# Cosformer attention and a gelu MLP on one core: batch 0's first chunk by halves, fp32 idle matmuls, a 128-column selector

## The chip, the core and the metric

The kernel runs on one core of a Trainium2 chip. A core has five engines that run side by side: TensorE (PE, matmuls; its weight loads are shown apart as PEld), VectorE (DVE), ScalarE (ACT), GpSimd (POOL) and SyncE (SP, which here only issues DMAs). PE reads SBUF and writes PSUM; DVE and ACT carry results from PSUM to SBUF. The metric is device time in microseconds, the median of several executions. Beside it stands one profiled execution, whose trace all views of the profile come from.

## What is computed

Eight batches of a linear attention with eight heads, 576 positions and head size 64, and then a two-layer MLP on the 4608 rows of the result. Cut to what matters:

```python
def phi(x, c, s):
    r = np.maximum(x, 0.0)
    return np.concatenate([r * c, r * s], axis=-1)
q_p, k_p = phi(q, cos_w, sin_w), phi(k, cos_w, sin_w)
kv = np.einsum('bhsf,bhsd->bhfd', k_p, v)
z = np.sum(k_p, axis=2)
num = np.einsum('bhsf,bhfd->bhsd', q_p, kv)
den = np.einsum('bhsf,bhf->bhs', q_p, z)[..., None] + 1e-06
x = (num / den).transpose(0, 2, 1, 3).reshape(4608, 512)
h = x @ w_in                       # 512 x 2048
g = h / (1.0 + np.exp(-1.702 * h))
out = g @ w_out                    # 2048 x 512
```

## The kernel before

The order of the instructions is written out by hand, and each engine takes its own in that order; the tile framework adds the semaphores. A tile name stands for a buffer out of a pool: PSUM has four buffers "mm" (pool pmm, one bank each) and two buffers "at" (pool pat, two banks each). A buffer is given again when its last reader is done.

Batch 0 has nothing to hide behind, and its steps stand at the end of the code (L355 to L435):

- SP issues four loads at the very start: k in two parts, then q in two parts (L62, L63). POOL waits for k's first part (the tiny copy into "gate" at L130), then issues v in two parts (heads 0 to 3 and 4 to 7, cast to bf16) and the first two of four parts of w_in (L132 to L134).
- idle(12) at L355 runs twelve matmuls on zeros before k lands; more of them stand between later steps.
- trig (L135) makes relu(x)cos and relu(x)sin of 64 positions, one instruction each, on DVE, on ACT, or, for q's last group, on POOL. There are nine groups j of k and of q. Groups 0 to 3 of q lie in its first loaded part.
- ksum(j) (L214) sums k over the positions: four matmuls with the selector "sel" of two columns. ksum_evac brings the sums to column 64 of "kvs".
- qturn_pe(c) turns two groups of q (128 positions, a chunk) on PE, and qevac(c) copies the result to qT, on DVE or ACT. Chunk 4 has one group.
- kv_mm(0, 2) and kv_mm(2, 4) (L202) make k times v for four heads each, 36 matmuls of 64 rows, into two "at" tiles; kv_evac copies them to kvs on DVE.
- den_early(0) makes chunk 0's denominators; num_mm(c) (L226) makes the numerators of eight heads, with the denominators in column 64 of each, into an "at" tile; num_div(c) on DVE adds 1e-6, takes the reciprocal and multiplies, into "xn".
- xturn_mm(c) turns xn on PE into the free columns of the same "at" tile, and xturn_evac(0, c) copies that on ACT to x. Chunk 4 goes by a DMA instead.
- part(c, fcs) makes the first w_in products of chunk c alone, four matmuls of 128 columns for each of the first four blocks fc of hidden units; gelu and the following blocks (mm1, 512 columns) come after all of them. The first is mm1(0, 4).

The other batches overlap their attention with the MLP of the batch before. SP, POOL, DVE and ACT take batch 1's loads and preparation behind batch 0's steps, in the same order as the code.

Of the kernel before, what the change touches and what calls it, by code (L numbers as in the profile page):

```python
# [9 lines left out]
F32 = mybir.dt.float32  # L10
BF16 = mybir.dt.bfloat16
AF = mybir.ActivationFunctionType
MUL = mybir.AluOpType.mult
# [6 lines left out]
def kernel(  # L20
# [40 lines left out]
    for t, src, cut in ((kf, k, 192), (qf0, q, 256)):  # L61
# [44 lines left out]

    win_r = moe_w_in.rearrange("(kc p) f -> p kc f", p=128)
    wout_r = moe_w_out.rearrange("(g p c) d -> p g c d", p=128, c=4)
    w_in_v = [t.rearrange("p k (f c) -> p k c f", c=4) for t in w_in_sb]

    def w_in_of(kc, fc):
        return w_in_v[fc // 4][:, kc, fc % 4, :]

    def load(t, src, b, eng=nc.gpsimd):
        eng.dma_start(out=t, in_=src_of(src, b))
# [5 lines left out]
                            in_=q[b, :, 512:S, :].rearrange("h p d -> p h d"))  # L121

    def load_win(g):
        nc.gpsimd.dma_start(out=w_in_sb[g], in_=win_r[:, :, ts(g, 512)])

    def load_wout(g):
        nc.gpsimd.dma_start(out=w_out_sb[:, ts(g, 4), :], in_=wout_r[:, g])
# [7 lines left out]
    def trig(dst, src, j, act=False, eng=nc.vector):  # L135
        i = src[:, :, ts(j, 64)]
        for cs, w in enumerate((cosw, sinw)):
            o = dst[:, j, :, ts(cs, 64)]
            if act:
                nc.scalar.activation(o, i, AF.Relu, scale=w[:, j:j + 1])  # L140
            else:
                eng.tensor_scalar(o, i, 0.0, w[:, j:j + 1], op0=MAX, op1=MUL)  # L142
# [24 lines left out]
    def qturn_pe(c, home=None):  # L167
        tp = pmm.tile([128, 2, NI, 128], BF16, name="mm") if home is None else home
        for j in range(2 * c, min(2 * c + 2, NS)):
            for i in range(NI):  # L170
                nc.tensor.transpose(tp[:, j % 2, i], qn0[:, j, i, :], ident)  # L171
        tps[c] = tp

    def qevac(c, act=False):
        n = min(2 * c + 2, NS) - 2 * c
        o = qT[:, :, ds(c * 128, n * 64)].rearrange("f h (j p) -> f j h p", j=n)
        i = tps.pop(c)[:, 0:n].rearrange("f j i (hh p) -> f j (i hh) p", hh=2)
        if act:
            nc.scalar.activation(o, i, AF.Copy)  # L179
        else:  # L180
            nc.vector.tensor_copy(o, i)  # L181
# [10 lines left out]
    st = {}  # L192
# [9 lines left out]
    def kv_mm(i0, i1, rhs, col, n):  # L202
        for i in range(i0, i1):
            for j in range(NS):
                for hh in range(2):
                    r = slice(hh * 64, hh * 64 + 64)
                    nc.tensor.matmul(st["kv", i][:, hh, ds(col, n)], kr[r, j, i, :], rhs(r, i, j),  # L207
                                     start=(j == 0), stop=(j == NS - 1))

    def kv_evac(i0, i1, n=65):  # L210
        o = st["kvs"][:, :, i0:i1, 0:n]
        nc.vector.tensor_copy(o, st["ps", i0].rearrange("p hh (i e) -> p hh i e", e=65)[:, :, :, 0:n])  # L212

    def ksum(j):  # L214
        if j == 0:
            st["z"] = pmm.tile([128, NI, 2], F32, name="mm")
        for i in range(NI):
            nc.tensor.matmul(st["z"][:, i], kr[:, j, i, :], sel, start=(j == 0 and i == 0),
                             stop=(j == NS - 1 and i == NI - 1))

    def ksum_evac():
        nc.vector.tensor_copy(st["kvs"][:, :, :, 64], st["z"].rearrange("f i hh -> f hh i"))

    nums = {}

    def num_mm(c):  # L226
        ps = pat.tile([128, 2, 512], F32, name="at")
        for h in range(H):
            i, hh = divmod(h, 2)
            nc.tensor.matmul(ps[:, h // 4, ds((h % 4) * 65, 65)], qT[:, h, ts(c, 128)],  # L230
                             st["kvs"][:, hh, i, 0:65], start=True, stop=True)
        nums[c] = [ps]

    def inv_of(d):
        den = small.tile([128, 2, 4], F32, name="den")
# [3 lines left out]
        return inv  # L239

    def den_early(c):
        d = pmm.tile([128, 2, 4], F32, name="mm")
        for h in range(H):
            nc.tensor.matmul(d[:, h // 4, h % 4:h % 4 + 1], qT[:, h, ts(c, 128)],
                             st["kvs"][:, h % 2, h // 2, 64:65], start=True, stop=True)
        return inv_of(d)

    def num_div(c, inv=None):
# [4 lines left out]
        xn = small.tile([128, 2, 4, 64], BF16, name="xn", bufs=4)  # L253
        nc.vector.tensor_tensor(xn, pv[:, :, :, 0:64],  # L254
                                inv.unsqueeze(3).to_broadcast([128, 2, 4, 64]), op=MUL)
        nums[c].append(xn)

    x = {}

# [9 lines left out]
    def xturn_mm(c):  # L269
        ps, xn = nums[c]  # L270
        xv = xn.rearrange("p a h e -> p (a h e)")
        for kc in range(KC):
            o = ps[:, kc // 2, ds(264 + (kc % 2) * 64, 64)].bitcast(BF16)
            nc.tensor.transpose(o, xv[:, ts(kc, 128)], ident)  # L274

    def xturn_evac(b, c):
        ps = nums.pop(c)[0]
        i = ps[:, :, 264:392].bitcast(BF16).rearrange("p a (k t) -> p a k t", k=2)
        o = x_of(b, c).rearrange("p (a k) t -> p a k t", a=2)
        nc.scalar.activation(o, i, AF.Copy)  # L280

    def xturn_dma(b, c):
# [5 lines left out]
    gT = {}  # L288
    hp = {}

    def mm1_part(b, fc, t0, t1):
        if t0 == 0:
            hp[fc] = pmm.tile([128, MT], F32, name="mm")
        for kc in range(KC):
            nc.tensor.matmul(hp[fc][:, t0:t1], w_in_of(kc, fc), x[b][:, kc, t0:t1],  # L295
                             start=(kc == 0), stop=(kc == KC - 1))

# [75 lines left out]
    ksum_evac()  # L373
    idle(1, w)
    qturn_pe(0)
    for j in (2, 3):
        trig(qn0, qf0, j, act=True)
    idle(2, w)
    qturn_pe(1)
    for j in (4, 5):  # L380
        trig(qn0, qf0, j)
    trig(qn0, qf0, 8, eng=nc.gpsimd)
    nc.gpsimd.tensor_copy(gate[0:1, 1:2], vb[0:1, 3, 0:1])
    load_win(2)
    load_win(3)
    kv_mm(0, 2, vb_rhs, 0, 64)
    qturn_pe(2)
    for j in (6, 7):
        trig(qn0, qf0, j, act=True)
    qevac(0)  # L390
    qevac(1)
    qevac(2, act=True)
    inv0 = den_early(0)
    kv_evac(0, 2, 64)
    kv_mm(2, 4, vb_rhs, 0, 64)
    kv_evac(2, 4, 64)
    qturn_pe(3)
    qevac(3, act=True)
    num_mm(0)
    num_div(0, inv0)  # L400
    num_mm(1)
    num_div(1)
    qturn_pe(4)
    qevac(4)
    idle(1)
    x_open(0)
    xturn_mm(0)
    xturn_evac(0, 0)
    num_mm(2)
    num_div(2)  # L410
    xturn_mm(1)
    xturn_evac(0, 1)

    def part(c, *fcs):
        for fc in fcs:
            mm1_part(0, fc, c * 128, c * 128 + 128)

    part(0, 0, 1, 2, 3)
    num_mm(3)
    num_div(3)  # L420
    xturn_mm(2)
    xturn_evac(0, 2)
    part(1, 0, 1, 2, 3)
    num_mm(4)
    num_div(4)
    xturn_mm(3)
    xturn_evac(0, 3)
    xturn_dma(0, 4)
    part(2, 0, 1, 2)
    part(3, 0, 1)  # L430
    part(2, 3)
    part(3, 2, 3)
# [150 lines left out]
```

## Time and profile before

| what | value |
|---|---|
| time of the kernel, median of 3 runs | 292.08 us (291.86 to 293.0) |
| the profiled execution: time | 292.75 us |
| its span, first to last instruction | 291.0 us |
| granted TensorE clock over the span | 1.000 |
| PE busy from 14.40 to 17.80 us | 2.39 of 3.40 us |
| PE busy from 17.80 to 21.70 us | 3.88 of 3.90 us |
| w_in's loads, issue to landing, least / median / most | 7.9 / 9.5 / 11.8 us |
| v's two loads of batch 0, issue to landing | 6.8 and 7.3 us |

A row of the timeline has the start, the time from the first start to the last end, the engine, the line, the operation with "output<-input", the shape and the number of instructions merged. A bracket at its end is the idle time of the engine before it and what ended it. Matmuls overlap, so the distance between two starts is what one costs, and not its duration. A row of the stage table has for each engine the busy time and the number of instructions; the figure after the engines is the share of full clock that PE was granted.

### The profile page before, as it was taken

What the parts mean: (1) busy time and instruction counts of PE and PEld (TensorE: products, weight loads), DVE (VectorE), ACT (ScalarE), POOL (GpSimd) and SP (SyncE); (2) the same over time, 40 slices, a digit from 0 to 9 for tenths busy, and PEclk for the clock granted to TensorE, in tenths of its full rate; (3) what the DMA queues carried; (4) which work ended last, traced back from release to release, by engine and by line L of the source; (5) the groups of instructions that cost most, each with busy time, mean ns of one, the idle gap of its engine ahead of it and who ended that gap; (6) DMA issues with size and microseconds to landing.
All of it is one profiled execution on the core that took longest, in us unless ns stands there. A gap on an engine that the chain in (4) does not pass through costs nothing.

```text
span 291.0 us, 5656 instructions
## 1 busy us (share of the span) xinstructions
PE 281.8 (97%) x2247; PEld 153.0 (53%) x2282; DVE 123.7 (43%) x356; ACT 133.1 (46%) x232; POOL 37.8 (13%) x71
## 2 busy tenths in 40 slices
PE   6989999999999999999999999999999999999995
PEld 2685475555555555555455545554555455544444
DVE  3872656912657354826582567156624200000000
ACT  6857564793157214721463136412651176751111
POOL 6560042301210011001100110011000100002000
PEclk9999999999999999999999999999999999999999
DMA  7999999982699877989797579846952600002322
GB/s 239 247 213 289 368 247 362 239 193 76 128 271 260 219 131 260 289 184 147 221 314 198 96 203 346 222 102 159 373 94 72 119 36 1 0 2 44 84 90 72
DMA packets 67770, 52.48 MB, mean 180 GB/s; under 512 B 47968, under 2 KB 57952, under 8 KB 67744
## 3 DMA queue, kind: packets, MB, share of 16 engines
q1 hardware_dynamic: 60320, 32.52, 47.0%
q0 software_dynamic: 7424, 19.60, 23.9%
q8 instruction: 18, 0.29, 0.4%
q14 instruction: 8, 0.07, 0.1%
HBM read 36.70 MB, written 9.44 MB: 159 GB/s over the span
## 4 chain that ended last, share of the span: by engine, by line
PE 91%; DMA 3%; ACT 2%; DVE 1%; issue 1%; SPq 1%; ACTq 0%
PE mm L332 42%; PE mm L295 37%; PE mm L312 5%; PE at L230 3%; PE at L207 3%; DMA qf<-in_q_dram 3%; ACT g L300 1%; PE at L274 1%; DVE qn L142 1%; DVE qT L181 0%; PE at L171 0%; ACT qT L179 0%; SPq L62 0%; DVE xn L254 0%; ACT xT L280 0%
## 5 line engine op out<-in xcount | busy, mean ns | idle before, releaser
L332 PE MATMUL mm<-w_out_sb,g 128*128 128x512 bf16 (+1 forms) x506 | 116.7, 372 | 1.3 <-issue 0.2
L295 PE MATMUL mm<-xT,w_in 128*128 128x512 bf16 (+1 forms) x551 | 111.9, 360 | 0.5
L300 ACT ACTIVATE g<-mm 128x512 bf16<-128x512 f32 x128 | 75.6, 598 | 31.0 <-PE mm L295 31.0
L295 PEld LDWEIGHTS <-w_in 128*128 128x128 bf16 x560 | 59.8, 113 | 50.9
L332 PEld LDWEIGHTS <-g 128*128 128x128 bf16 x528 | 48.6, 98 | 49.1
L336 ACT ACTIVATE ysb<-mm 128x512 f32<-128x512 f32 (+1 forms) x37 | 21.7, 586 | 105.9 <-PE mm L332 103.0
L340 POOL DMA_DIRECT2D out_dram<-ysb x39 | 21.3, 547 | 204.7 <-ACT ysb L336 204.7
L142 DVE TENSOR_SCALAR kr<-kf,cosw 128x256 bf16<-128x256 f32 x64 | 22.6, 353 | 29.4 <-DMA kf<-in_k_dram 29.4
L254 DVE TENSOR_TENSOR xn<-at,inv 128x512 bf16<-128x512 f32 x40 | 27.7, 691 | 1.9 <-PE at L230 0.4
L142 DVE TENSOR_SCALAR kr<-kf,sinw 128x256 bf16<-128x256 f32 x64 | 22.2, 347 | 0.0
L212 DVE CAST kvs<-at 128x520 bf16<-128x520 f32 (+1 forms) x9 | 5.6, 634 | 33.7 <-PE at L207 33.7
L236 DVE TENSOR_SCALAR den<-at 128x8 f32<-128x8 f32 x39 | 6.5, 166 | 31.4 <-PE at L230 31.4
L230 PEld LDWEIGHTS <-qT 128*128 128x128 bf16 x320 | 14.8, 97 | 8.8 <-issue 0.8
L230 PE MATMUL at<-kvs,qT 128*128 128x65 bf16 x320 | 16.1, 193 | 0.7 <-ACT xT L280 0.7
L155 DVE TENSOR_SCALAR qn<-qf,sinw 128x512 bf16<-128x512 f32 (+1 forms) x30 | 14.4, 480 | 0.0
L155 DVE TENSOR_SCALAR qn<-qf,cosw 128x512 bf16<-128x512 f32 (+1 forms) x30 | 14.3, 476 | 0.0
L312 PE MATMUL mm<-xt,w_in 128*128 128x512 bf16 x63 | 13.9, 379 | 0.1
L332 PE MATMUL mm<-w_out_sb,gl_t 128*128 128x512 bf16 x63 | 13.9, 379 | 0.1
L313 ACT ACTIVATE gl_t<-mm 128x512 bf16<-128x512 f32 x16 | 9.6, 597 | 4.2 <-PE mm L312 4.2
L207 PEld LDWEIGHTS <-kr 64*128 64x128 bf16 x576 | 9.3, 94 | 2.8 <-issue 2.5
L312 PEld LDWEIGHTS <-w_in 128*128 128x128 bf16 x64 | 7.2, 113 | 6.6
L332 PEld LDWEIGHTS <-gl_t 128*128 128x128 bf16 x64 | 6.3, 98 | 7.5
(63 smaller groups left out, 114.5 us busy)
## 6 DMA issues: line engine op xcount, KB each, us to landing
kf<-in_k_dram SPq DMA_DIRECT2D x5, 1152.0 KB, 6.7
vf<-in_v_dram SPq DMA_DIRECT2D x5, 1152.0 KB, 9.5
qf<-in_q_dram SPq DMA_DIRECT2D x5, 1024.0 KB, 5.9
out_dram<-ysb POOLq DMA_DIRECT2D x20, 256.0 KB, 3.9
out_dram<-ysb POOLq DMA_DIRECT2D x19, 128.0 KB, 3.2
kf<-in_k_dram POOLq DMA_DIRECT2D x2, 1152.0 KB, 11.3
vf<-in_v_dram POOLq DMA_DIRECT2D x2, 1152.0 KB, 15.7
w_in<-in_moe_w_in_dram POOLq DMA_DIRECT2D x4, 512.0 KB, 9.5
```

Source lines behind the costliest of these rows:

```text
L142: eng.tensor_scalar(o, i, 0.0, w[:, j:j + 1], op0=MAX, op1=MUL)
L155: nc.vector.tensor_scalar(o, i, 0.0, sc, op0=MAX, op1=MUL)
L207: nc.tensor.matmul(st["kv", i][:, hh, ds(col, n)], kr[r, j, i, :], rhs(r, i, j), start=(j == 0), stop=(j == NS - 1))
L230: nc.tensor.matmul(ps[:, h // 4, ds((h % 4) * 65, 65)], qT[:, h, ts(c, 128)], st["kvs"][:, hh, i, 0:65], start=True, stop=True)
L254: nc.vector.tensor_tensor(xn, pv[:, :, :, 0:64], inv.unsqueeze(3).to_broadcast([128, 2, 4, 64]), op=MUL)
L295: nc.tensor.matmul(hp[fc][:, t0:t1], w_in_of(kc, fc), x[b][:, kc, t0:t1], start=(kc == 0), stop=(kc == KC - 1))
L300: nc.scalar.activation(g, hp.pop(fc), AF.Gelu_apprx_sigmoid)
L312: nc.tensor.matmul(hps, w_in_of(kc, fc), xt[:, kc, :], start=(kc == 0), stop=(kc == KC - 1))
L313: nc.scalar.activation(gl_t[:, fc, :], hps, AF.Gelu_apprx_sigmoid)
L332: nc.tensor.matmul(yp[t, c0][:, c0:c1], w, w_out_sb[:, fc, c0:c1], start=(fc == 0), stop=(fc == FC - 1))
L336: nc.scalar.activation(ysb[:, c0:c1], yp[t, c0][:, c0:c1], AF.Identity)
L340: eng.dma_start(out=dst[:, c0:c1], in_=ysb[p0:p0 + n, c0:c1])
```

## The change

- The idle matmuls at the start are three on fp32 zeros (a 128x128 tile read four times over) in place of twelve on bf16 zeros; the later idles read the same bytes as bf16. Of these one stays, before qturn_pe(1); nine others go.
- The selector has 2 x 64 columns in place of 2, so that a sum stands 64 times in PSUM; ksum_evac reads the first of each.
- w_in's first part is loaded as two tiles, each with half of the input rows.
- Chunk 0 is done by halves of four heads: numerators of heads 0 to 3 right after kv_mm(0, 2), then kv_mm(2, 4), division, turn and copy of the first half, then the second; the first two blocks' w_in products of the first half stand ahead of the second half.
- qevac(0) stands on DVE between q's groups 4 and 5, q's group 7 on ACT behind qevac(1), and qevac(3) on DVE in place of ACT. den_early also makes chunk 1's denominators, in the tile of chunk 0's.
- Chunk 4 of q is turned into free columns of chunk 2's "at" tile (qturn_last) and copied on ACT (qevac_last), after num_mm(2) and ahead of num_div(2).
- The w_in products of chunks 0 to 3 stand in a new order around num_mm(3), num_mm(4) and the turns.

```diff
-    warm = const.tile([128, 512], BF16)
-    nc.vector.memset(warm, 0.0)
+    warm32 = const.tile([128, 128], F32)
+    nc.vector.memset(warm32, 0.0)
+    warm = warm32.bitcast(BF16)
...
-    sel = const.tile([128, 2], BF16)
+    sel = const.tile([128, 2, 64], BF16)
     nc.vector.memset(sel, 0.0)
     for hh in range(2):
-        nc.vector.memset(sel[hh * 64:hh * 64 + 64, hh:hh + 1], 1.0)
+        nc.vector.memset(sel[hh * 64:hh * 64 + 64, hh], 1.0)
...
-    w_in_sb = [one.tile([128, KC, 512], BF16, name=f"w_in{g}") for g in range(4)]
+    w_in0 = [one.tile([128, 2, 512], BF16, name=f"w_in0{u}") for u in "ab"]
+    w_in_sb = [one.tile([128, KC, 512], BF16, name=f"w_in{g}") for g in range(1, 4)]
...
+    def qturn_last(c_home):
+        for i in range(NI):
+            o = nums[c_home][0][:, i // 2, ds(264 + (i % 2) * 64, 64)].bitcast(BF16)
+            nc.tensor.transpose(o, qn0[:, NS - 1, i, :], ident)
+
+    def qevac_last(c_home):
+        nc.scalar.activation(qT[:, :, ds(512, 64)].rearrange("f (a h) p -> f a h p", a=2),
+                             nums[c_home][0][:, :, 264:392].bitcast(BF16).rearrange(
+                                 "f a (h p) -> f a h p", h=4), AF.Copy)
...
-    def idle(n, w=None):
+    def idle(n, w=None, t=warm):
         if w is None:
             w = pmm.tile([128, 512], F32, name="mm")
         for _ in range(n):
-            nc.tensor.matmul(w, warm[:, 0:128], warm, start=True, stop=True)
+            nc.tensor.matmul(w, t[:, 0:128], t[:, 0:128].unsqueeze(1).to_broadcast([128, 4, 128]),
+                             start=True, stop=True)
         return w
...
-    w = idle(12)
+    w = idle(3, t=warm32)
...
-    for j in (0, 1, 2):
-        ksum(j)
-    for j in (3, 6, 4, 7, 5):
-        idle(1, w)
-        ksum(j)
-    idle(1, w)
-    ksum(8)
+    for j in (0, 1, 2, 3, 6, 4, 7, 5, 8):
+        ksum(j)
```

num_mm, num_div, xturn_mm and xturn_evac get bounds for the half (heads h0 to h1, halves a0 to a1 of the tile), and mm1_part gets bounds k0 to k1 of the input blocks. From the sums on, batch 0's order was this, up to the mm1 of block 4:

```python
ksum_evac(); idle(1, w); qturn_pe(0); trig q 2, 3 (ACT); idle(2, w); qturn_pe(1)
trig q 4, 5; trig q 8 (POOL); load_win(2); load_win(3)
kv_mm(0, 2); qturn_pe(2); trig q 6, 7 (ACT); qevac(0); qevac(1); qevac(2, act=True)
inv0 = den_early(0); kv_evac(0, 2); kv_mm(2, 4); kv_evac(2, 4)
qturn_pe(3); qevac(3, act=True); num_mm(0); num_div(0, inv0); num_mm(1); num_div(1)
qturn_pe(4); qevac(4); idle(1); x_open(0); xturn_mm(0); xturn_evac(0, 0)
num_mm(2); num_div(2); xturn_mm(1); xturn_evac(0, 1)
part(0, 0, 1, 2, 3); num_mm(3); num_div(3); xturn_mm(2); xturn_evac(0, 2)
part(1, 0, 1, 2, 3); num_mm(4); num_div(4); xturn_mm(3); xturn_evac(0, 3); xturn_dma(0, 4)
part(2, 0, 1, 2); part(3, 0, 1); part(2, 3); part(3, 2, 3)
```

and becomes this:

```python
ksum_evac(); trig q 8 (POOL); load_win(2); load_win(3)
qturn_pe(0); trig q 2, 3 (ACT); trig q 4; qevac(0); trig q 5; trig q 6 (ACT)
idle(1, w); qturn_pe(1); qevac(1, act=True); trig q 7 (ACT)
kv_mm(0, 2); kv_evac(0, 2); inv0 = den_early(0); qturn_pe(2)
num_mm(0, 0, 4); kv_mm(2, 4); num_div(0, inv0, 0, 1); kv_evac(2, 4)
x_open(0); xturn_mm(0, 0, 1); xturn_evac(0, 0, 0, 1); inv1 = den_early(1); qevac(2, act=True)
num_mm(0, 4, 8); num_mm(1); mm1_part(0, fc, 0, 128, 0, 2) for fc in (0, 1)
num_div(0, inv0, 1, 2); num_div(1, inv1); xturn_mm(0, 1, 2); xturn_evac(0, 0, 1, 2)
qturn_pe(3); qevac(3); xturn_mm(1); xturn_evac(0, 1)
num_mm(2); qturn_last(2); qevac_last(2); num_div(2)
mm1_part(0, fc, 0, 128, 2, 4) for fc in (0, 1); part(0, 2, 3)
num_mm(3); num_div(3); part(1, 0); xturn_mm(2); xturn_evac(0, 2); part(1, 1, 2, 3)
part(2, 0); xturn_mm(3); xturn_evac(0, 3); num_mm(4); num_div(4); xturn_dma(0, 4)
part(2, 1, 2); part(3, 0, 1); part(2, 3); part(3, 2, 3)
```

More of the change, by code (lines that the diff above doesn't have):

```diff
@@ L108 @@
     wout_r = moe_w_out.rearrange("(g p c) d -> p g c d", p=128, c=4)
+    w_in0_v = [t.rearrange("p k (f c) -> p k c f", c=4) for t in w_in0]
     w_in_v = [t.rearrange("p k (f c) -> p k c f", c=4) for t in w_in_sb]
     def w_in_of(kc, fc):
-        return w_in_v[fc // 4][:, kc, fc % 4, :]
+        if fc < 4:
+            return w_in0_v[kc // 2][:, kc % 2, fc, :]
+        return w_in_v[fc // 4 - 1][:, kc, fc % 4, :]
     def load(t, src, b, eng=nc.gpsimd):
@@ L123, in load_win @@
     def load_win(g):
-        nc.gpsimd.dma_start(out=w_in_sb[g], in_=win_r[:, :, ts(g, 512)])
+        if g == 0:
+            for u in range(2):
+                nc.gpsimd.dma_start(out=w_in0[u], in_=win_r[:, ds(2 * u, 2), 0:512])
+        else:
+            nc.gpsimd.dma_start(out=w_in_sb[g - 1], in_=win_r[:, :, ts(g, 512)])
     def load_wout(g):
@@ L221, in ksum_evac, with num_mm @@
     def ksum_evac():
-        nc.vector.tensor_copy(st["kvs"][:, :, :, 64], st["z"].rearrange("f i hh -> f hh i"))
+        nc.vector.tensor_copy(st["kvs"][:, :, :, 64], st["z"][:, :, :, 0].rearrange("f i hh -> f hh i"))
     nums = {}
-    def num_mm(c):
-        ps = pat.tile([128, 2, 512], F32, name="at")
-        for h in range(H):
+    def num_mm(c, h0=0, h1=H):
+        if h0 == 0:
+            nums[c] = [pat.tile([128, 2, 512], F32, name="at")]
+        ps = nums[c][0]
+        for h in range(h0, h1):
             i, hh = divmod(h, 2)
@@ L241, in den_early @@
     def den_early(c):
-        d = pmm.tile([128, 2, 4], F32, name="mm")
+        if c == 0:
+            st["den"] = pmm.tile([128, 2, 2, 4], F32, name="mm")
+        d = st["den"][:, c]
         for h in range(H):
@@ L267, in x_of, with xturn_mm, xturn_evac @@
         return xt[:, :, ts(b, 64)] if c == 4 else x[b][:, :, ts(c, 128)]
-    def xturn_mm(c):
+    def xturn_mm(c, a0=0, a1=2):
         ps, xn = nums[c]
         xv = xn.rearrange("p a h e -> p (a h e)")
-        for kc in range(KC):
+        for kc in range(2 * a0, 2 * a1):
             o = ps[:, kc // 2, ds(264 + (kc % 2) * 64, 64)].bitcast(BF16)
             nc.tensor.transpose(o, xv[:, ts(kc, 128)], ident)
[L276 to L279, printed above, removed]
+    def xturn_evac(b, c, a0=0, a1=2):
+        ps = nums[c][0] if a1 < 2 else nums.pop(c)[0]
+        i = ps[:, a0:a1, 264:392].bitcast(BF16).rearrange("p a (k t) -> p a k t", k=2)
+        o = x_of(b, c).rearrange("p (a k) t -> p a k t", a=2)[:, a0:a1]
         nc.scalar.activation(o, i, AF.Copy)
@@ L289, with mm1_part @@
     hp = {}
-    def mm1_part(b, fc, t0, t1):
-        if t0 == 0:
+    def mm1_part(b, fc, t0, t1, k0=0, k1=KC):
+        if t0 == 0 and k0 == 0:
             hp[fc] = pmm.tile([128, MT], F32, name="mm")
-        for kc in range(KC):
+        for kc in range(k0, k1):
             nc.tensor.matmul(hp[fc][:, t0:t1], w_in_of(kc, fc), x[b][:, kc, t0:t1],
@@ L373 @@
     ksum_evac()
[L374 to L381, printed above, removed]
     trig(qn0, qf0, 8, eng=nc.gpsimd)
@@ L385 @@
     load_win(3)
+    qturn_pe(0)
+    for j in (2, 3):
+        trig(qn0, qf0, j, act=True)
+    trig(qn0, qf0, 4)
+    qevac(0)
+    trig(qn0, qf0, 5)
+    trig(qn0, qf0, 6, act=True)
+    idle(1, w)
+    qturn_pe(1)
+    qevac(1, act=True)
+    trig(qn0, qf0, 7, act=True)
     kv_mm(0, 2, vb_rhs, 0, 64)
+    kv_evac(0, 2, 64)
+    inv0 = den_early(0)
     qturn_pe(2)
[L388 to L391, printed above, removed]
-    qevac(2, act=True)
[L393 to L400, printed above, removed]
-    num_mm(1)
[L402 to L410, printed above, removed]
+    num_mm(0, 0, 4)
+    kv_mm(2, 4, vb_rhs, 0, 64)
+    num_div(0, inv0, 0, 1)
+    kv_evac(2, 4, 64)
+    x_open(0)
+    xturn_mm(0, 0, 1)
+    xturn_evac(0, 0, 0, 1)
+    inv1 = den_early(1)
+    qevac(2, act=True)
+    num_mm(0, 4, 8)
+    num_mm(1)
+    q3 = pmm.tile([128, 2, NI, 128], BF16, name="mm")
+    for fc in (0, 1):
+        mm1_part(0, fc, 0, 128, 0, 2)
+    num_div(0, inv0, 1, 2)
+    num_div(1, inv1)
+    xturn_mm(0, 1, 2)
+    xturn_evac(0, 0, 1, 2)
+    qturn_pe(3, q3)
+    qevac(3)
     xturn_mm(1)
     xturn_evac(0, 1)
+    num_mm(2)
+    qturn_last(2)
+    qevac_last(2)
+    num_div(2)
     def part(c, *fcs):
@@ L416, in part @@
             mm1_part(0, fc, c * 128, c * 128 + 128)
-    part(0, 0, 1, 2, 3)
+    for fc in (0, 1):
+        mm1_part(0, fc, 0, 128, 2, 4)
+    part(0, 2, 3)
     num_mm(3)
     num_div(3)
+    part(1, 0)
     xturn_mm(2)
     xturn_evac(0, 2)
-    part(1, 0, 1, 2, 3)
+    part(1, 1, 2, 3)
+    part(2, 0)
+    xturn_mm(3)
+    xturn_evac(0, 3)
     num_mm(4)
     num_div(4)
-    xturn_mm(3)
-    xturn_evac(0, 3)
     xturn_dma(0, 4)
-    part(2, 0, 1, 2)
+    part(2, 1, 2)
     part(3, 0, 1)
```

13 lines of the change are left out of this document (6 added, 7 removed).

## The prediction

> **What bounds the kernel now.** I read four views of the profile: the page's first parts, the table of stages (busy time by stretch), the timeline of TensorE (PE), and the timeline of the other engines.
>
> ```profile
> PE 281.8 (97%) x2247; PEld 153.0 (53%) x2282; DVE 123.7 (43%) x356; ACT 133.1 (46%) x232; POOL 37.8 (13%) x71
> ...
> 14.40:17.80 3.40, 2.39 (x51) 2.16 (x49) 2.78 (x8) 2.22 (x3) 3.40 (x6) 1.00 1.24 207
> 17.80:21.70 3.90, 3.88 (x77) 3.78 (x76) 2.40 (x7) 1.90 (x4) 1.14 (x3) 1.00 1.25 213
> 21.70:291.00 269.30, 264.17 (x1958) 140.19 (x1988) 109.65 (x310) 118.22 (x204) 24.85 (x44) 1.00 0.69 176
> ```
>
> PE is busy nearly all the time, and from 17.8 us on it has hardly a hole. So the change, which touches only batch 0's opening, is worth what it does to the moment when PE becomes full. In the stage table the second number of a row is PE's busy time; the 14.40 row has the last large hole.
>
> ```profile
> 11.38 0.71 PE L207 MATMUL at<-vb,kr 64*128 64x64 bf16 x36
> 12.02 0.62 PE L171 MATMUL mm<-ident,qn 128*128 128x128 bf16 x8
> 12.83 0.35 PE L244 MATMUL mm<-kvs,qT 128*128 128x1 bf16 x8 [0.19 <-DVE qT L181]
> ...
> 15.42 0.40 PE L274 MATMUL at<-ident,xn 128*128 128x128 bf16 x4 [0.32 <-DVE xn L254]
> 16.51 0.40 PE L230 MATMUL at<-kvs,qT 128*128 128x65 bf16 x8 [0.69 <-ACT xT L280]
> 16.74 0.39 PE L274 MATMUL at<-ident,xn 128*128 128x128 bf16 x4
> 16.97 1.06 PE L295 MATMUL mm<-xT,w_in 128*128 128x128 bf16 x16
> 17.86 0.41 PE L230 MATMUL at<-kvs,qT 128*128 128x65 bf16 x8
> 18.13 0.40 PE L274 MATMUL at<-ident,xn 128*128 128x128 bf16 x4
> ```
>
> The brackets are PE's holes: 0.19, 0.32 and 0.69 us, all waits for chunk 0's way through DVE and ACT. That way begins with q's second half and its POOL neighbour:
>
> ```profile
> 10.67 0.35 DVE L142 TENSOR_SCALAR qn<-qf,cosw 128x256 bf16<-128x256 f32 x1 [0.84 <-DMA qf<-in_q_dram]
> 10.94 0.57 DVE L142 TENSOR_SCALAR qn<-qf,sinw 128x256 bf16<-128x256 f32 x1
> 11.43 0.34 DVE L142 TENSOR_SCALAR qn<-qf,cosw 128x256 bf16<-128x256 f32 x1
> 11.69 0.49 DVE L142 TENSOR_SCALAR qn<-qf,sinw 128x256 bf16<-128x256 f32 x1
> 12.10 1.27 DVE L181 COPY qT<-mm 128x1024 bf16<-128x1024 bf16 x2
> ...
> 39.19 0.69 DVE L181 COPY qT<-at 128x1024 bf16<-128x1024 bf16 x1 [1.63 <-PE at L171]
> 39.91 2.11 ACT L179 ACTIVATE qT<-at 128x1024 bf16<-128x1024 bf16 x2 [1.77 <-DVE qT L181]
> ```
>
> The last two rows matter most for the forecast. Both copies read halves of one PSUM tile ("at") that PE had finished at 39.16, yet ACT began only at 39.91, released by DVE: two readers of one tile go one after the other.
>
> **The start up to 11.4 us: nothing.** Twelve bf16 idle matmuls become three fp32 ones, six idles between k's sums go, and the 36 sums get 128 columns in place of 2. The trace has no fp32 matmul. If one costs a single bf16 pass, the three take 3 x 0.43 = 1.3 us at the opening spacing (12 in 4.2 us, the first seven 0.43 apart); if four passes, 3 x 1.7 = 5.1. I take four, nearest to the twelve they replace: they end near 5.3, when the first k is ready (5.28). The Trainium skill, "FP8 and Floating Point Precision", section TensorE Precision Notes, also gives true fp32 four passes; no run here shows it yet. A sum of 128 columns costs what a 128-column transpose costs (L171, 0.056 apart), so one j is 0.22 us, and the last j starts when ACT frees it (9.35) and ends by 9.58, as before with its idle. The second half of chunk 1's transposes still waits for ACT's qn (10.89) and the first kv product for v's landing (11.34), so its start stays at 11.38. POOL issues three w_in loads where two stood, some 0.8 us more; its next work waits for q until 10.67, which covers that, as it was done by 7.7. The software queue lands in order (v 11.34 and 12.72, w_in0 15.26), so w_in0's first half should land near 14.0; it is needed at 15.0. Without the split the wait would be 0.2 us.
>
> **The chain from 10.67, step by step.** I use start-to-start distances and add 0.04 to 0.06 us for each hand-over (L171 out at 15.82, ACT 15.86; DVE done 15.37, PE 15.42) and 0.16 for a matmul's way out.
>
> 1. DVE: one pair of qn (0.76, row 10.67 to 11.43), then qevac(0) 11.43 to 12.10 (before it ended 12.77), then the second pair (0.67) to 12.78, then kv_evac(0,2), 0.37 (L212's 128x256 copy), to 13.07.
> 2. PE: den_early(0) at 12.16 (before 12.83). The later half of qturn_pe(2) waits for qn until 12.84. num_mm of heads 0 to 3 at 13.13 (half of L230's 0.24), then kv_mm(2,4), 36 in 0.52, to 13.80.
> 3. The half division has no row: between 0.37 (128x256 copy) and 0.69 (L254 whole). I take 0.42, near the same-sized copy: 13.45 to 13.87. The half turn is at 13.93. The half copy on ACT lies between 0.29 (its smallest row, cosw) and 0.60 (L280 whole); 512 elements take 0.60 and 1024 take 1.02, so 256 take about 0.38: 14.24 to 14.62.
> 4. num_mm of heads 4 to 7 writes the tile that ACT just read, so it waits until 14.67 (hole 0.43); num_mm(1) and the four first w_in matmuls run to 15.25. DVE: kv_evac(2,4) to 14.40, inv1, other half of xn 14.99 to 15.41, xn(1) to 16.02. PE: xturn_mm(0) rest 15.47, qturn_pe(3), and xturn_mm(1) at 16.08. **Before, it was at 16.74: here the change is 0.66 us ahead.**
> 5. num_mm(2) 16.30, then chunk 4's four transposes into the same "at" tile, out at 16.93. ACT copies xT(1) 16.50 to 17.10, then these transposes (128x512, 0.60) to about 17.60. DVE's den(2) reads that tile too, and in the built order it stands behind this ACT copy. So den, reciprocal, xn (0.16, 0.20, 0.69, with gaps 1.13 as from 16.94 to 18.07) run 17.64 to 18.77, and xturn_mm(2) starts at 18.83; **before 18.13**. PE has from 16.76 only 12 w_in matmuls (0.67), num_mm(3) (0.24) and four more (0.22): done 17.89, hole 0.94. This hole doesn't hang on the steps before: 0.17 + 0.04 + 0.60 + 0.04 + 1.13 + 0.06 is 2.0, the cover 1.13.
> 6. xturn_mm(2) 18.83, ACT's xT(2) to 19.85, part(2, 0) waits for it (hole 0.18); xturn_mm(3) 20.12, xT(3) to 21.14; part(3, 0) at 21.19 (hole 0.16). Before, it was at 20.58. The same 20 matmuls follow in both.
>
> Sum: 21.19 - 20.58 = +0.61 us. Counted by PE's holes after 11.4: before 0.19 + 0.07 + 0.32 + 0.69 + 0.18, with the idle in the 0.32's place 0.2 more, near 1.8; after 0.13 + 0.22 + 0.07 + 0.43 + 0.22 + 0.05 + 0.94 + 0.18 + 0.16 = 2.4. Both ways say +0.6. The gain of the early half is real, and the new wait in step 5 takes more back.
>
> On that wait the Trainium skill, "PSUM — Partial Sum Buffer", section on bank collisions, says that reads of one bank by ScalarE and VectorE must be kept apart too. By that rule the order is needed, and the sum stays; rows 39.19 and 39.91 agree (0.03 us between end and start).
>
> The profiled run took 292.75 us (span 291.0, 1.75 around it), 0.67 above the median of 292.08. So I expect 293.36 on its basis, **292.7 us** on the median's.
>
> **Bounds.** Low: half division 0.37, half copy 0.29, second qn pair without POOL beside it 0.53: -0.28, so +0.3. High: 0.69, 0.60 and 0.98 (both instructions at the slow 0.49): +0.27 + 0.22 + 0.31 up to step 4, and +0.27 for the second half division: +1.7. Own range of the forecast 292.3 to 293.8.
>
> **Rivals.**
> - *The delay is swallowed later.* Some later wait with a fixed time would eat the 0.6. For it: the last stage row has 5.1 us without PE, though matmul records are missing there. Against it: the named holes after 22 us are near 0.2, and k, w_out and q of batch 1 land two to five us ahead of their use. 292.1.
> - *Faster.* Step 4's lead of 0.66 survives, because ACT takes chunk 4's copy ahead of its turn or den(2) isn't held by it. Then xn(2) follows num_mm(2) directly: DVE is free of qevac(3) at 16.96, xn(2) ends near 18.1 in place of 18.77, and with the low bounds the sum is 0.61 - 0.67 - 0.28 - 0.2 (shorter second holes): 291.5. For it: before, den always followed its num_mm within 0.23. Against: the order of the built program and row 39.91.
> - *Slower: the clock.* PE runs its first seven idles 0.43 apart and later ones 0.22, so the full clock comes at 4.2 us, after 3 us of steady work. If three fp32 matmuls are too short (one pass, over at 2.5) or count as little work, or the sums without idles between them are too thin to hold it, PE enters the chain at half speed. Between 11.4 and 14.8 it has 2.7 us of work there, some 0.9 of which would hide in holes: +1.8 on top of 0.6, 294.5. It decides once the clock is still half at 11.4. Against it: by four passes PE works without a break until 5.3, and from 7.59 to 11.0 its work is 22 x 0.056 + 1.2 = 2.4 us, close to the 2.5 of before.
>
> **Numbers.** Forecast 0.62, swallowed 0.16, faster 0.13, clock 0.09. Around 0.5% (1.5 us) is what a measurement of this kernel tells from no change, since the three runs lie 1.1 us apart: the forecast lies inside it but for its upper end. Faster by over 0.5% needs the faster rival twice over: 0.04. Slower by over 0.5%: the clock and 0.03 of the forecast's upper end, 0.12. The rest, 0.84, is the same. Range: from 291.3, just under the faster rival, to 293.9; below it 0.06, above 0.11.
>
> **What would show it** (lines of the changed kernel). den(2) at L256 on DVE released by ACT's L198 and starting near 17.6; a hole near 0.9 us before the turn of chunk 2 (L296); xturn_mm(1) earlier than 16.74; part(3,0) near 21.2; PE's clock full before 5.3, with three fp32 matmuls ending there. The forecast is wrong if den(2) starts with num_mm(2)'s end, if PE has new holes behind 22 us, or if 128-column sums lie 0.11 apart.

## The result, and the profile after

| what | before | after |
|---|---|---|
| median of 19 runs each | 292.16 us (291.56 to 293.11) | 292.94 us (292.73 to 293.63) |
| ratio after / before | | 1.0032, 95% interval 1.0024 to 1.0041 |
| the profiled execution: time, span | 292.75, 291.0 us | 292.94, 291.2 us |
| q's and v's second parts land at | 10.64, 12.72 us | 9.78, 12.39 us |
| first 512-column matmul (mm1(0, 4)) at | 21.69 us | 21.61 us |
| from there to the end | 269.35 us | 269.54 us |

The change makes the kernel 0.8 us slower, which is 0.3%. The two profiled executions differ by only 0.2 us, because the one of before had its loads land late. That is why I compare two distances that depend far less on when loads land: **the opening**, from v's second landing to the first 512-column matmul, and **the tail**, from that matmul to the end.

The page of the changed kernel and its table of stages (for each engine busy time and number of instructions, then granted clock):

```profile
PE 282.7 (97%) x2242; PEld 153.9 (53%) x2275; DVE 124.0 (43%) x356; ACT 133.5 (46%) x234; POOL 38.6 (13%) x72
...
14.40:17.80 3.40, 2.88 (x56) 2.52 (x52) 2.41 (x6) 1.85 (x4) 3.10 (x5) 1.00 1.24 207
17.80:21.61 3.81, 3.47 (x60) 3.27 (x61) 2.30 (x7) 1.88 (x4) 1.06 (x2) 1.00 1.24 209
21.61:291.15 269.54, 264.33 (x1958) 140.17 (x1989) 109.53 (x310) 118.19 (x204) 24.51 (x44) 1.00 0.67 176
```

From 14.40 to 17.80 PE was busy for 2.39 us before and is for 2.88 now: the halves do fill the old hole. From 17.80 on there was no hole before (3.88 of 3.90), and now 0.34 us are missing. The timeline of PE shows where:

```profile
13.29 0.34 PE L266 MATMUL mm<-kvs,qT 128*128 128x1 bf16 x8
13.92 0.52 PE L251 MATMUL at<-kvs,qT 128*128 128x65 bf16 x12 [0.29 <-ACT xT L302]
...
15.39 0.40 PE L296 MATMUL at<-ident,xn 128*128 128x128 bf16 x4
15.62 0.41 PE L251 MATMUL at<-kvs,qT 128*128 128x65 bf16 x8
15.87 0.39 PE L195 MATMUL at<-ident,qn 128*128 128x128 bf16 x4
...
17.12 0.28 PE L317 MATMUL mm<-xT,w_in0b 128*128 128x128 bf16 x2
18.13 0.40 PE L296 MATMUL at<-ident,xn 128*128 128x128 bf16 x4 [0.73 <-DVE xn L277]
```

Chunk 1 is turned at 15.39 (before 16.74), chunk 2 at 18.13 as before: the lead is used up in one hole of 0.9 us (17.23 to 18.13 by starts). Part of these differences is that the loads landed earlier. Counted from v's second landing, and set against e5 (the kernel before once more, see the experiments), chunk 1's turn comes after 3.00 us in place of 3.65, and chunk 2's after 5.74 in place of 5.04: a lead of 0.65 becomes a delay of 0.70. DVE and ACT tell why:

```profile
15.56 0.69 DVE L190 COPY qT<-mm 128x1024 bf16<-128x1024 bf16 x1 [0.23 <-PE mm L180]
16.94 0.17 DVE L256 TENSOR_SCALAR den<-at 128x8 f32<-128x8 f32 x1 [0.69 <-ACT qT L198]
```

```profile
15.82 0.60 ACT L302 ACTIVATE xT<-at 128x512 bf16<-128x512 bf16 x1 [0.33 <-PE at L296]
16.32 0.59 ACT L198 ACTIVATE qT<-at 128x512 bf16<-128x512 bf16 x1
```

DVE is free at 16.25 and chunk 2's numerators have been out since 16.03. It begins chunk 2's denominators only at 16.94, when ACT is through with chunk 4's copy (L198) out of the same tile. And one place behind 22 us is new:

```profile
39.84 1.02 ACT L188 ACTIVATE qT<-at 128x1024 bf16<-128x1024 bf16 x1 [1.92 <-DVE qT L190]
41.22 1.94 ACT L188 ACTIVATE qT<-at 128x1024 bf16<-128x1024 bf16 x2 [0.36 <-ACT qT L188]
```

Before, these three copies ran without a gap:

```profile
39.91 3.03 ACT L179 ACTIVATE qT<-at 128x1024 bf16<-128x1024 bf16 x3 [1.77 <-DVE qT L181]
```

Now the second begins 0.36 us late, although what it reads is ready.

### The profile page after: what moved, and what is told of

Its sections match the earlier page's. It is cut to its first block, busy times and chain, and to the rows that moved or that the text cites. A ratio compares the mean times of both kernels' runs of the same rounds, so it can differ in the third digit from the quotient of the medians.

```text
span 291.2 us, 5650 instructions
## 1 busy us (share of the span) xinstructions
PE 282.7 (97%) x2242; PEld 153.9 (53%) x2275; DVE 124.0 (43%) x356; ACT 133.5 (46%) x234; POOL 38.6 (13%) x72
## 3 DMA queue, kind: packets, MB, share of 16 engines
HBM read 36.70 MB, written 9.44 MB: 158 GB/s over the span
## 4 chain that ended last, share of the span: by engine, by line
PE 91%; DMA 3%; ACT 3%; issue 1%; DVE 1%; ACTq 0%; POOL 0%; DVEq 0%
PE mm L354 42%; PE mm L317 36%; PE mm L334 5%; PE at L251 3%; PE at L226 3%; DMA vb<-in_v_dram 2%; ACT g L322 1%; DMA kf<-in_k_dram 1%; ACT qT L188 1%; PE at L296 1%; PE at L180 0%; DVE xn L277 0%; ACT xT L302 0%; PE mm L180 0%; DVE qT L190 0%
## 5 line engine op out<-in xcount | busy, mean ns | idle before, releaser
L317 PE MATMUL mm<-xT,w_in 128*128 128x512 bf16 x377 | 83.8, 379 | 0.4
L317 PEld LDWEIGHTS <-w_in 128*128 128x128 bf16 x384 | 43.4, 113 | 39.2
L277 DVE TENSOR_TENSOR xn<-at,inv 128x512 bf16<-128x512 f32 (+1 forms) x41 | 27.7, 678 | 1.7 <-PE at L251 0.2
L317 PE MATMUL mm<-xT,w_in0b 128*128 128x512 bf16 (+1 forms) x87 | 20.2, 320 | 0.1
L317 PE MATMUL mm<-xT,w_in0a 128*128 128x512 bf16 (+1 forms) x87 | 20.3, 320 | 0.0
L317 PEld LDWEIGHTS <-w_in0a 128*128 128x128 bf16 x88 | 9.1, 114 | 6.1
L317 PEld LDWEIGHTS <-w_in0b 128*128 128x128 bf16 x88 | 9.0, 113 | 5.7
```

The lines of the kernel that those rows point to most:

```text
L277: nc.vector.tensor_tensor(nums[c][1][:, a0:a1], pv[:, a0:a1, :, 0:64], inv[:, a0:a1].unsqueeze(3).to_broadcast([128, a1 - a0, 4, 64]), op=MUL)
```

## The experiments

Opening and tail as defined above, from each run's profiled execution. Runs made together share a chip and the runs of before; the ratio is to before.

| run | ratio, 95% interval | opening | tail |
|---|---|---|---|
| before, its first profile | | 8.97 | 269.35 |
| before, unchanged (e5) | 0.9995, 0.9983 to 1.0006 | 8.59 | 269.57 |
| after | 1.0032, 1.0024 to 1.0041 | 9.22 | 269.54 |
| before with the shared tile (e4) | 1.0032, 1.0016 to 1.0049 | 9.44 | 269.32 |
| after, chunk 4 in its own tile (e1) | 1.0018, 1.0010 to 1.0027 | 8.74 | 269.55 |
| e1 with one part moved (e2) | 1.0015, 1.0006 to 1.0023 | 8.48 | 269.53 |
| after, ACT's list shifted (e6) | 1.0026, 1.0015 to 1.0038 | 9.24 | 269.30 |
| e2, ACT's list shifted (e9) | 0.9997, 0.9985 to 1.0008 | 8.45 | 269.31 |
| before with the new start (e3) | 1.0016, 1.0007 to 1.0025 | 8.60 | 269.32 |
| before, fp32 idles only (e7) | 0.9992, 0.9981 to 1.0003 | 8.60 | 269.30 |
| before, wide selector only (e10) | 1.0010, 0.9996 to 1.0024 | 8.89 | 269.31 |
| before, w_in's first part split (e11) | 1.0009, 0.9994 to 1.0024 | 9.05 | 269.37 |
| e9 with before's start (e8) | 1.0018, 1.0000 to 1.0037 | 8.98 | 269.30 |
| the same again (e12) | 1.0009, 0.9996 to 1.0022 | 8.97 | 269.31 |

### The shared tile alone (e4), and taken away (e1)

e4 puts only chunk 4's new place into the kernel before, with its copy on ACT and ahead of num_div(2), as the change has it (before, that copy is on DVE). e1 takes the place out of the changed kernel and leaves the copy on ACT.

```diff
 # e4, against before
-    qturn_pe(4)
-    qevac(4)
...
     num_mm(2)
+    qturn_last(2)
+    qevac_last(2)
     num_div(2)
 # e1, against after
-    qturn_last(2)
-    qevac_last(2)
+    qturn_pe(4)
+    qevac(4, act=True)
```

> The kernel before with chunk 4 of q turned into chunk 2's buffer at and copied on ACT ahead of num_div(2), as the change does, and nothing else. Theory (the shared buffer): den(2) waits for that copy, some 0.8 us later than before (16.9), and the hole goes through to the end: 0.7 to 0.9 us slower, 292.9 to 293.1. Rival (the start): no change, 292.1 to 292.3.

> The changed kernel with one thing undone: chunk 4 of q is turned into a buffer mm of its own (and still copied on ACT, at the same place) in place of the free columns of chunk 2's buffer at. Theory (the shared buffer): den(2) no longer waits for ACT's copy and starts with the end of qevac(3), some 0.7 us earlier; the block part(0, 3) now waits for that copy to free its buffer, about 0.4 us, so the hole of 0.9 us before chunk 2's turn shrinks to about 0.4 us in all and the kernel loses about 0.3 us against before in place of 0.8: near 292.5. Rival (the start costs it: three fp32 matmuls, the full clock at 5.4 us, wide sums): den(2) doesn't set the pace, and the time stays at 292.9 to 293.0.

Measured: e4 292.64 us and e1 292.39 us beside 291.78 us of before on that chip. So e4 is 0.86 slower than before, as the theory said, and e1 is 0.6 slower, where the theory said 0.3. In e4, DVE's timeline shows the wait that the changed kernel has:

```profile
15.01 0.69 DVE L264 TENSOR_TENSOR xn<-at,inv 128x512 bf16<-128x512 f32 x1
17.09 0.17 DVE L246 TENSOR_SCALAR den<-at 128x8 f32<-128x8 f32 x1 [1.39 <-ACT qT L189]
```

The opening grows from 8.59 to 9.44 by nothing but this, +0.85 us. In e1 the same step on DVE no longer waits, and another wait has come up on PE (DVE row first, PE rows below it):

```profile
16.20 0.16 DVE L256 TENSOR_SCALAR den<-at 128x8 f32<-128x8 f32 x1
```

```profile
16.45 0.27 PE L317 MATMUL mm<-xT,w_in0b 128*128 128x128 bf16 x2
16.99 0.27 PE L317 MATMUL mm<-xT,w_in0a 128*128 128x128 bf16 x2 [0.26 <-ACT qT L188]
```

The denominators start at 16.20 in place of 16.94, as soon as DVE is free. But the next w_in products, part(0, 3), take the "mm" buffer in which chunk 4 now stands and wait for its copy, and chunk 3's numerators queue behind them. So the opening shortens by 0.48 of the 0.74 us that DVE gained.

### One part moved (e2)

```diff
 # against e1
-    part(0, 2, 3)
+    part(0, 2)
     num_mm(3)
     num_div(3)
     part(1, 0)
+    part(0, 3)
```

> As the run before, and part(0, 3) stands behind num_mm(3) and part(1, 0), so that nothing waits for chunk 4's copy. Theory (the shared buffer): chunk 2's turn comes about 0.7 us earlier than in the changed kernel, with a hole of some 0.2 us ahead of it; time within 0.1 us of before, 292.2. Rival (the start): 292.9 to 293.0.

Measured: 292.10 us, which is 0.3 over before and not within 0.1 of it, as the theory said. The opening is 8.48, another 0.26 us shorter, and for the first time under the 8.59 of before. By the whole time the step from e1 to e2 is 0.3 us, and the intervals of the ratios overlap.

### ACT's list shifted (e6, e9)

The trace has 380 rows for ACT in the changed kernel; these are the instructions that the page counts and the waits between them. The 64th, 192nd and 320th (at 41.22, 125.41 and 239.07 us) begin 0.32 to 0.34 us behind the end of the row ahead, a wait that was over, where such a pair is else 0.05 apart. They are 128 rows apart. In e1 and e2, which have as many rows, the same three are late by as much. Before has three rows fewer, and its 64th row is a copy that waits 1.8 us for PE anyway. So two tiny instructions were added ahead of k's landing (the trace shows one row more, as one wait is gone):

```diff
     nc.scalar.activation(gl, halfpi, AF.Gelu_apprx_sigmoid)
+    nc.scalar.activation(gl, halfpi, AF.Gelu_apprx_sigmoid)
+    nc.scalar.activation(gl, halfpi, AF.Gelu_apprx_sigmoid)
```

> The changed kernel with two more one-column instructions on ACT ahead of k's landing, so that the 64th entry of ACT's list, which began 0.36 us late in the changed kernel, is no longer the copy of batch 1's turned q at 41 us. Theory (every 128th entry on ACT begins about 0.3 us late, and in the changed kernel this falls on a copy that TensorE waits for): the gap of 0.36 us ahead of the copy is gone, the stretch from the first whole up-projection step to the end is 269.35 us instead of 269.54, and the time is 0.2 us under the changed kernel's, near 292.7. Rival (the late start belongs to that copy, for example because its source comes late): the copy is late again, 292.9.

> The run with chunk 4 in a tile of its own and the moved part, kept as it was with the changed kernel's start, plus the two one-column instructions on ACT. That run gave ratio 1.0015 to before, and the two instructions took 0.24 us out of the stretch behind 22 us. Theory (the two add): ratio 1.0007, some 0.2 us over before, stretch to the end 269.30 us, chunk 3's numerators follow at once on the parts ahead of them, as in that run. Rival (the two instructions on ACT bring the hole of 0.70 us ahead of chunk 3's numerators that the combined kernel showed): that hole again, and ratio 1.0018 or more.

Measured: e6 292.66 us beside 291.84 of before, e9 291.90 beside 291.93. ACT's copies in e6, and then the tail of e6 in the table of stages:

```profile
39.88 3.03 ACT L190 ACTIVATE qT<-at 128x1024 bf16<-128x1024 bf16 x3 [1.91 <-DVE qT L192]
```

```profile
21.66:290.95 269.29, 266.00 (x1991) 140.21 (x1988) 109.52 (x310) 118.24 (x204) 24.45 (x44) 1.00 0.67 176
```

The gap is gone and the tail is 0.24 us shorter, with the same work in it. PE had waited for that copy: its chunk 4 of batch 1 is turned at 43.21 in the changed kernel and at 43.02 in e6, although e6's opening ended 0.05 later (the changed kernel's row first):

```profile
43.21 0.38 PE L180 MATMUL at<-ident,qn 128*128 128x128 bf16 x4
```

```profile
43.02 0.39 PE L182 MATMUL at<-ident,qn 128*128 128x128 bf16 x4
```

By the whole time, ratio 1.0026 against 1.0032, the difference is within the intervals; the rows show it, the medians alone would not.

e9 puts the three together. Chunk 3's numerators and chunk 2's turn on its PE:

```profile
16.48 0.27 PE L319 MATMUL mm<-xT,w_in0b 128*128 128x128 bf16 x2
16.59 0.41 PE L253 MATMUL at<-kvs,qT 128*128 128x65 bf16 x8
...
17.40 0.40 PE L298 MATMUL at<-ident,xn 128*128 128x128 bf16 x4
```

Chunk 2's turn is at 17.40, 0.73 us ahead of the changed kernel. The time is that of before. So with three things mended, the shared tile, the order around it and ACT's late entry, the loss is gone. By the profiled executions they are worth 1.00 us together (opening and tail against the changed kernel), more than the 0.82 that the change lost against e5's opening and the tail of before's first profile; the rest is a gain on before that the losses had hidden.

### The start (e3, e7, e10)

e3 is the kernel before with the new start (fp32 idles, no idles between the sums, wide selector), e7 only the fp32 idles, e10 only the wide selector.

> The kernel before with the change's start alone: three fp32 idle matmuls for twelve, no idles between k's sums, the selector of 128 columns. Theory (the shared buffer): the chain from q's second half is untouched, so the same time, 292.1 to 292.3; the first sums start some 0.6 us later and nothing follows from it. Rival (the start): 292.6 to 293.0, with the first kv product or chunk 0's turn later against q's landing.

> The kernel before with nothing changed but the twelve bf16 idle matmuls ahead of k, which become three fp32 ones (the idles between k's sums stay, and the two-column selector too). The first of the two halves of the start, whose whole cost was 0.28 us in the run with the new start alone (ratio 1.0016). Theory A (the late end of the fp32 idles, 5.9 us against 5.3, holds the sums up, and with them TensorE's list): 292.1, that is the whole of it. Theory B (the wide sums, or the idles left out between them, cost it): the time of before, 291.8, within 0.1 us. The first sum at 5.9 us by both.

> The kernel before with the wide selector alone: k's sums of 128 columns for two, idles as in before. The new start as a whole gave 1.0016, its fp32 idles alone 0.9992. Theory A (the wide sums cost it, by holding up the copy of the sums on VectorE and q's rotation behind it): ratio 1.0010 to 1.0020. Theory B (the idles that were left out between the sums cost it, or it is the landing of the loads that differed): 1.0000 within 0.0010, and the last sum about 0.1 us later behind k's landing than the 2.67 us of before.

Measured: e3 292.06 beside 291.78, e7 291.76 beside 291.84, e10 292.44 beside 291.93. The fp32 idles cost nothing, although in e7 the first sum came at 6.39 us, later than the 5.9 that was expected, as the full clock was granted only at 6.79. In the changed kernel they show as six records for three matmuls:

```profile
1.11 4.93 PE L368 MATMUL mm<-warm 128*128 128x512 f32 x6 [1.11 <-DVE warm L76]
5.88 0.83 PE L237 MATMUL mm<-sel,kr 128*128 128x128 bf16 x12
7.21 2.10 PE L237 MATMUL mm<-sel,kr 128*128 128x128 bf16 x24 [0.50 <-DVE kr L151]
```

The records are 0.85 us apart, so one fp32 matmul is 1.7, four times the 0.43 of a bf16 one at that clock. In e10 the wide sums with the old idles between them make PE the bound:

```profile
8.74 0.38 PE L346 MATMUL mm<-warm 128*128 128x512 bf16 x1
8.95 0.83 PE L218 MATMUL mm<-sel,kr 128*128 128x128 bf16 x8
9.62 0.38 PE L346 MATMUL mm<-warm 128*128 128x512 bf16 x1
...
10.71 0.61 PE L171 MATMUL mm<-ident,qn 128*128 128x128 bf16 x8
11.25 0.23 PE L207 MATMUL at<-vb,kr 64*128 64x64 bf16 x4
```

An idle and four wide sums take 0.44 us, the last sum is 3.22 us behind k's landing (2.67 in e5), and the first product with v starts 0.35 behind v's landing at 10.90. In e5 and in the changed kernel it starts within 0.05 of it, the latter because most of its idles are gone. So in the changed kernel's profiled execution the whole start holds nothing up; e10's medians are 0.5 us apart, though its interval just takes in no change. What e3's 1.0016 comes from stays open: its profiled execution has the opening and the tail of before. It isn't alone: by the medians e1, e2 and e3 are each some 0.25 to 0.3 us slower than their openings and tails say, and e4, measured with them, is not. In e3 PE begins to turn chunk 1 4.01 us behind k's second landing, but the kernel before does so after 3.78 us in its first profile and 4.04 in e5, so that tells nothing.

### When the loads land (e5, e11)

> The kernel before, unchanged: what its profiled execution looks like when it is near its median. Theory (the profiled execution of before, 292.75 us, was one in which q and v landed late): here q's second part lands near 9.7 and v's near 12.1 to 12.4 us instead of 10.64 and 12.72, the first matmul of step 4 of the up-projection's first sweep starts near 21.0 to 21.3 us instead of 21.69, the stretch from there to the end stays 269.3 to 269.4, and the time is 291.8 to 292.2 us. Rival (the landings are the same and before's other time was lost behind 22 us): q's second part again at 10.6 and the stretch to the end longer than 269.4.

```diff
 # e11, against before
-    w_in_sb = [one.tile([128, KC, 512], BF16, name=f"w_in{g}") for g in range(4)]
+    w_in0 = [one.tile([128, 2, 512], BF16, name=f"w_in0{u}") for u in "ab"]
+    w_in_sb = [one.tile([128, KC, 512], BF16, name=f"w_in{g}") for g in range(1, 4)]
...
-        nc.gpsimd.dma_start(out=w_in_sb[g], in_=win_r[:, :, ts(g, 512)])
+        if g == 0:
+            for u in range(2):
+                nc.gpsimd.dma_start(out=w_in0[u], in_=win_r[:, ds(2 * u, 2), 0:512])
+        else:
+            nc.gpsimd.dma_start(out=w_in_sb[g - 1], in_=win_r[:, :, ts(g, 512)])
```

> The kernel before with nothing changed but w_in's first part, loaded in two tiles of 256 KB. In five profiled executions of kernels that load it so, v's second part landed at 12.39 to 12.45 us every time, in five that load it whole at 11.92 to 12.90. Theory A (the two smaller loads take a share of the transfers from q and v, so that the early landings near 11.9 are gone): no run under 291.8, median 292.0 to 292.3. Theory B (the loads do not meet): the time of before, 291.8 within 0.1, its lowest near 291.5.

Measured: e5 291.86 us (291.53 to 292.70), its profiled execution 292.70 with q at 9.98 and v at 12.82. So it was another late one, and the expected near-median picture did not come. Its tail is 0.2 us longer as well: batch 1's two casts of v took 1.94 us on DVE, 1.58 in e7, and PE's products with v took 1.52 and not 1.26. What it does show is that the same code spreads over 1.2 us. In e7, v lands at 11.92 and the time is 291.61; in e5 it lands 0.90 later, and the time is 1.09 longer, with 0.27 of that in the tail.

e11: 292.47 us (291.66 to 293.70) beside 291.93. Theory A said that no run would be under 291.8, and one is at 291.66; theory B said 291.8. Neither is borne out. In e12, which loads it in two tiles as well, v landed at 12.21, so the narrow range of the first five doesn't hold. Here v landed at 12.53, and the extra in the opening has another place:

```profile
17.18 0.28 PE L303 MATMUL mm<-xT,w_in0b 128*128 128x128 bf16 x2
17.30 0.19 PE L238 MATMUL at<-kvs,qT 128*128 128x65 bf16 x1
17.79 0.37 PE L238 MATMUL at<-kvs,qT 128*128 128x65 bf16 x7 [0.30 <-issue]
```

PE stops for 0.5 us between the first and the second of chunk 3's eight numerator matmuls, where it waits for no other engine ("issue").

### The parts put together with before's start (e8, e12)

> The changed kernel without what the runs before found to cost: chunk 4 is turned in a tile of its own, one up-projection part of chunk 0 is moved behind chunk 3's numerators, k's sums and the idles are as in the kernel before, and ACT has two more one-column instructions ahead of k. By the sum of the runs: 292.10 (own tile and order) less 0.2 (ACT's late entry) less 0.28 (the start) is 291.6, which is 0.2 under before's 291.8 on the same chip; the half copies and half divisions are then worth their 0.2 us. Rival (these costs lie beside one another and do not add): 291.8 to 292.1, the same as before.

> The combined kernel again. Its first profile showed TensorE idle for 0.70 us ahead of chunk 3's numerators, where the same list had no hole without the changed start; the instruction that these numerators wait for had ended 0.76 us before. Theory A (a mishap of that execution): the hole is not there, chunk 2's turn is near 17.4 us and not 17.95, the profiled run is near 291.9. Theory B (it belongs to the list): the hole is there again, and the median stays at 292.3.

Measured: e8 292.30 us (291.91 to 295.01) beside 291.84, e12 292.19 beside 291.93. The sum of the parts is missed by 0.7 us, and theory B of e12 holds: the hole is there both times. PE, and then ACT, in e12:

```profile
16.25 0.28 PE L319 MATMUL mm<-xT,w_in0b 128*128 128x128 bf16 x2
17.01 0.40 PE L253 MATMUL at<-kvs,qT 128*128 128x65 bf16 x8 [0.49 <-ACT qT L190]
```

```profile
15.64 0.60 ACT L304 ACTIVATE xT<-at 128x512 bf16<-128x512 bf16 x1 [0.33 <-PE at L298]
16.14 0.59 ACT L190 ACTIVATE qT<-mm 128x512 bf16<-128x512 bf16 x1
```

The program makes chunk 3's numerators wait for the upper ACT row, which ended at 16.24; the profile's guess, the lower one, isn't what they wait for. They start 0.77 us later. In e8, e11 and e12 the stop lies at the same place in PE's list: entry 447 has run, entry 448 has not (each matmul counts as two entries, a weight load and a matmul), though the instructions there differ. Shortly before, the queue that the page calls "instruction" moved its first 16 KB packet in these executions:

| run | packet, start to end | PE goes on at entry 448 | behind the packet's end |
|---|---|---|---|
| e12 | 14.62 to 15.59 us | 17.01 us | 1.42 us |
| e8 | 15.05 to 16.03 us | 17.26 us | 1.23 us |
| e11 | 15.46 to 16.43 us | 17.79 us | 1.36 us |

Before, e4, e5 and e10, which count alike as they have no fp32 matmul, come there at 17.38 to 17.89 us, 1.43 to 2.02 behind their packet's end, and show no stop. With an fp32 matmul counted as its two records, the other seven come there 1.27 to 1.96 behind, and do not stop either. With before's start, e8 and e12 have more idle matmuls ahead of that entry than e9, and so come to it earlier. All fourteen fit one reading: PE runs out of fetched instructions there, and gets on some 1.2 to 1.4 us after the packet. The Trainium skill, "Runtime: NRT & Kernel Launch", section Instruction fetch mechanics, has each engine's list fetched in blocks of 16 KiB, 256 instructions, over a DMA queue, and calls the cost of crossing a block mostly hidden. The packet's size agrees, the 128 rows between ACT's stalls do not, and entry 448 is no multiple of 256 as the rows are counted here. The cost, 0.5 to 0.7 us on PE and 0.3 on ACT, was not hidden here. That the packet is the cause is argued from these rows; no run moved it by itself.

## Why the prediction was right

The forecast was +0.6 us, inside 0.5%; measured were +0.78 us between the medians and a ratio of 1.0032. It was right by its own steps, and short by one thing.

- **Step 5, the shared tile: right.** den(2) released by ACT's L198, a hole of 0.94 foreseen and 0.90 found. The smaller holes of step 6 are 0.18 and 0.16 by starts, as foreseen. e4 gives the wait by itself: +0.85 us.
- **Steps 1 to 4, the early half: right.** The half copy (0.38) and the half division (0.42) took what was chosen between the bounds. The head of the chain was another, though: the forecast starts from q's landing and DVE's work on it, while the profile's chain here starts from v's first landing (10.96) and runs through PE's products. DVE was done with q just as these came out (kv_evac at 11.82, with no gap before it), so that both heads gave nearly the same time; that is luck. All later steps stand a constant 0.7 us ahead of the forecast, as the loads landed earlier in this execution (us):

| step | forecast | measured | difference |
|---|---|---|---|
| second half's numerators, step 4 | 14.67 | 13.92 | -0.75 |
| xturn_mm(1), step 4 | 16.08 | 15.39 | -0.69 |
| den(2), step 5 | 17.64 | 16.94 | -0.70 |
| xturn_mm(2), step 5 | 18.83 | 18.13 | -0.70 |
| xturn_mm(3), step 6 | 20.12 | 19.43 | -0.69 |
| part(3, 0), step 6 | 21.19 | 20.50 | -0.69 |

- **The sum: +0.61 foreseen, +0.63 found** in the opening (9.22 against 8.59 us), once both are counted from v's landing, with before taken from e5 and e7 (8.59 and 8.60), where the opening waits for v. In the first profile of before q came later still, at 10.64, and held it to 8.97. That the two sums agree to 0.02 is partly luck: with the loads that the forecast assumed, its openings are 9.58 and 8.97, and the measured ones are shorter by 0.36 and 0.38. By the clock times of the two profiled executions it would have looked like a gain of 0.08.
- **The count by holes: added up wrongly.** The prediction's holes before, with the idle, make 1.65 and not near 1.8. Against 2.40 that is +0.75, so the second way did not say +0.6. The sum by steps is the one that held.
- **Rows 39.19 and 39.91: they show more than was read from them.** The two copies read different banks of their tile (at_homes gives each chunk one of the two), and still go one after the other, in all fourteen profiles. So the order goes by the tile here, and not by the bank or the columns. For step 5 this changes nothing, as chunk 4's copy and den(2) read both banks.
- **The start up to 11.4 us at nothing: right, with a detail off.** Four passes of fp32 agreed. They end at 5.9 and not at 5.3, and the full clock comes at 5.4 us and not before 5.3; the sums then wait for k, so nothing follows. The w_in half expected near 14.0 landed at 13.67.
- **Missed: the tail.** I named new holes behind 22 us as a sign against the forecast, and there is one: ACT's late entry, +0.19 us here and 0.24 by e6. It comes from the number of instructions on ACT's list, which the prediction did not count. 0.63 and 0.19 make 0.82, beside the 0.78 measured. So close a fit is luck too, as the median of before was 291.78 to 291.93 in the later comparisons and 292.16 here.
- **The rivals.** Nothing swallowed the delay: the tail is longer and not shorter. The clock stayed full from 5.4 us on. The faster rival's condition, den(2) not held by the copy, is what e1 and e2 built; its price was too high, since with it and the better order the opening gains 0.11 us on before (8.48 against 8.59), not the 0.6 that the rival took. Why e9, with an opening shorter by 0.14, is not faster than before in the medians stays open; when the loads landed is known for the profiled executions alone.

## What to carry to other kernels

A free corner of a tile isn't free if another engine still has to read the rest: two readers of one tile go one after the other, whichever part of it they read, and the copy put there held the next chunk for 0.85 us. Compare openings from the landing that they wait for, not from the start, when loads spread by a microsecond. And when an edit changes how many instructions an engine has, look behind the edit for a stall that has moved onto an instruction that someone waits for.

## What the runs showed of the hardware

- ACT began every 128th row of its list, waits counted, 0.3 us late where nothing else made that row wait (three rows each in the changed kernel, e1 and e2), and one row of shift took the stall off the path.
- PE stopped for 0.5 to 0.7 us at one fixed entry of its list in the three executions that came there 0.5 to 0.9 us after the instruction queue's packet had landed, and in none of the other eleven, which came there 1.27 us or more after it.
- The profile put PE's stop down to ACT in e8 and e12, and to "issue" in e11: the releaser named is a guess, and the wait in the program can rule it out.
- An fp32 matmul of 512 columns shows as two records of 0.85 us at the low opening clock.
- The landing of v's second part spread from 11.92 to 12.90 us over seven profiled executions of kernels that start as before or nearly so, and the whole time with it.
